# A chunked attention, mixture and MLP kernel: the first block's norm in earlier ticks, its later steps placed one by one, and a new order of the prologue

## The chip, the cores and the metric

The kernel runs on one core of one Trainium2 chip. The metric is the device time of one launch in microseconds, the median of several runs. The engines are named as in the profile: PE is TensorE (PEld its weight loads), DVE is VectorE, ACT is ScalarE, POOL is GpSimd, SP issues the DMAs.

## What is computed

The inputs are q, k, v of shape (8, 8, 576, 64) in float32, four experts' projections, a gate, a gain and two MLP weights in float64. Three stages follow each other; the reference, cut to what matters:

```python
# 1: attention within chunks of 64 positions, 8 heads
scores = 1/sqrt(64) * q_c @ k_c^T;  attn = softmax(scores);  x = attn @ v_c      # x: (8, 576, 512)
# 2: four single-head causal attention experts over 576 positions, top 2 of 4 weighted by a gate
logits = x @ w_gate;  w = softmax of the two largest
for e in range(4):
    a = softmax(causal(1/8 * (x @ wq[e]) @ (x @ wk[e])^T))
    out += (weight of e, or 0) * (a @ (x @ wv[e]) @ wo[e])
# 3: layer norm and MLP with a residual
xn = (out - mean) / sqrt(var + 1e-6) * g_ln
y = out + relu(xn @ w_ch1) @ w_ch2                                                # w_ch1: 512 x 2048
```

## The kernel before, in words

The 4608 rows are 36 tiles of 128 (`NT`). A **tick** `s` works on several tiles at once: the chunk attention of tile `s` (`chunk_scores`, `chunk_shift`, ...), the projections of a finished group of three tiles (`proj_group`), and the causal attention of tile `g = s - 6` in steps spread over three ticks. Ticks 6 to 36 do all of it, ticks 37 to 43 only what is left of the causal attention. Before tick 6 stands the **prologue**, the string `PRO` of L662, which loads the first six tiles and the projection weights, and keeps PE running with dummy products (`warm`, L92: `w40` and `w14`).

Every matmul operand of stages 2 and 3 is split in two float32r parts, a high one (a copy on ACT) and a low one (a subtraction on DVE or POOL), and three products are summed.

Within prologue and ticks nothing is scheduled: each engine gets its instructions in the order in which the code names them, and the code names them by the tables `PRO` and `PLAN` (L565), a letter for each step. For the steps of a tick: `S0`, `S1` scores (PE, L374), `D0`, `D1` mask and maximum (DVE, L392), `E0`, `E1` exp (ACT, L397), `L` sums (DVE, L405 to L407), `W` weighing (POOL, L414), and one tick later `T` transposes (PE, L425) whose results ACT and DVE copy to `pTa` (L427, L429), one more tick later `O` values (PE, L444), `Z` and `z` the high and low part of their result (`zh`, ACT and `zl`, DVE, both L447), `Y` the output projection (PE, L454, which needs `zl`), `y` its copy and store to the DRAM tile `xs`. `P` is a step of the projections (PE, L260 and L287), `a` and `v` their high and low parts. In the prologue: `c` chunk scores, `N` shift (DVE), `n` exp (ACT), `R` sums (DVE), `r` scaling (POOL), `K`, `k` transposes and their copy, `V` values, `H`, `X` the high and low part of x; `c`, `h`, `l`/`p` before a part's name (`v1`, `k0`, ...) load a half of a weight, make its high part, and its low part on DVE or POOL.

Stage 3 works by blocks of four tiles with seven products for each pair of hidden chunks (a Strassen-like scheme, L838). Block 0's input is made by `norm` for each of its two halves (load from `xs`, statistics, square root, scaling in place, transposes into `xt`), `sums` (four differences of quarters of `xt`), `operand` (seven operands `x7_1` to `x7_7`, high on ACT at L795, low on DVE at L796) and `split_w1` for the first two weight tiles `w1u0` and `w1u1` (L739, L740). All of that is one generator, `begin` (L799), of which the letter `F` in ticks 37 to 42 takes the next step. Block 1's norm stands later in the code, outside any table; its instructions are placed by the scheduler and land in ticks 38 to 40, as soon as block 0's transposes have freed the two buffers `xc`. The first five products of stage 3 (`lead_in`) are the letter `M` in ticks 42 and 43. From there to the end PE runs products back to back.

Buffers that matter here: `ps` and `pss` are PSUM pools with two and three buffers; `xc` has two.

Of the kernel before, what the change touches and what calls it, by code (L numbers as in the profile page):

```python
# [22 lines left out]
def tile_kernel(ctx, tc, dims, qkt, vt, wqt, wkt, wvt, wo, g_ln, w_ch1, w_ch2, out):  # L23
# [638 lines left out]
    PRO = ("L0 w40 c0 w14 L1 N0 cv1 c1 L2 cv0 n0 N1 R0 r0 n1 c2 hv1 K0 R1 r1 k0 N2 V0 hv0 lv1 n2 L3 K1 R2 c3 H0 k1 d2 V1 "  # L662
# [42 lines left out]
    E_ = mybir.EngineType  # L705
    ALL = {E_.PE, E_.DVE, E_.Activation, E_.Pool}
    with tc.manual_schedule(engines=ALL):
        for op in PRO.split():
            start_up(op)
        nc.sync.dma_start(gk, g_ln.rearrange("(f p) -> p f", p=128))  # L710
        bg(LA)
        for s in range(LA, MID):
            tick(s)
    early.close()

# [528 lines left out]
```

## Time and profile before

| | us |
|---|---|
| median of 3 runs | 1206.86 (1206.44 to 1208.41) |
| the profiled execution | 1207.36 |
| its span | 1205.6 |
| PE busy in the span | 1175.2 (97%) |
| DVE, ACT, POOL busy | 908.5, 579.3, 284.3 |
| prologue: to the first scores of tick 6 | 41.26 |
| tick 38 ends on PE at | 427.96 |
| first product of stage 3 on PE at | 466.31 |

The profiled execution is 0.5 us above the median. Its span is 1.76 us short of its time. PE is busy nearly throughout, so the table is to be read by stages: the gaps of PE are at the beginning (first 75 us) and between 428 and 466 us. A busy PE isn't always at its peak: its clock is granted at one of two levels, and the views by window give the mean (1.00 is 2.4 GHz, 0.50 is 1.2 GHz).

### The profile page before, as it was taken

Reading aid. Unit: us, or ns where it says so; the run is one execution under the profiler, and the core shown is the slowest. Engines: PE = TensorE matmul, PEld = TensorE weight load, DVE = VectorE, ACT = ScalarE, POOL = GpSimd, SP = SyncE. Lnnn points to the kernel's source line nnn. Section 1 sums busy time; section 2 is a strip of 40 time slices with the busy share of each in tenths; the row PEclk is TensorE's granted clock in tenths of the full one; section 3 lists DMA queues with packets and bytes.
Section 4 is the critical chain, followed back from the end, with each engine's and each line's share of the span. In section 5 each row is a group of like instructions: output and inputs, shape, how many; then the busy total and the mean of one; then the engine's idle time right before and its main releaser. Section 6 shows DMA issues by size and latency. Waiting matters only on the chain.

```text
span 1205.6 us, 29148 instructions
## 1 busy us (share of the span) xinstructions
PE 1175.2 (97%) x11838; PEld 1126.8 (93%) x11838; DVE 908.5 (75%) x1827; ACT 579.3 (48%) x1099; POOL 284.3 (24%) x490
## 2 busy tenths in 40 slices
PE   8899999999999979999999999999999999999998
PEld 7789988998988867999999999999999999999998
DVE  5888888888888785877765776556898777877782
ACT  3565656666666675534433433345454334333340
POOL 3345444535454362122111211210000000000000
PEclk8999999999999989999999999999999999999999
DMA  7343434343431233765555555558875455545521
GB/s 271 120 135 128 148 113 146 130 131 133 143 128 52 77 114 118 277 194 191 172 173 179 170 182 182 182 148 273 285 247 172 143 169 162 158 158 160 172 80 44
DMA packets 95733, 191.69 MB, mean 159 GB/s; under 512 B 8560, under 2 KB 41840, under 8 KB 94704
## 3 DMA queue, kind: packets, MB, share of 16 engines
q1 hardware_dynamic: 95600, 189.83, 48.1%
q8 instruction: 93, 1.52, 0.5%
q14 instruction: 40, 0.33, 0.1%
HBM read 118.50 MB, written 71.30 MB: 157 GB/s over the span
## 4 chain that ended last, share of the span: by engine, by line
PE 86%; DVE 9%; ACT 2%; POOL 1%; issue 1%; DMA 1%; ACTq 0%; POOLq 0%; DVEq 0%
PE bb L838 17%; PE bb L1069 16%; PE ad L838 13%; PE ad L1069 12%; PE pp L260 7%; PE oa_ps L444 3%; PE pv L287 3%; PE y_ps L454 3%; PE tp L425 3%; PE sp L374 3%; PE tp L778 1%; PE sx_ps L168 1%; PE pT_ps L194 1%; DVE P L392 1%; PE sx_ps L204 1%
## 5 line engine op out<-in xcount | busy, mean ns | idle before, releaser
L838 PE MATMUL bb<-x,w1u 128*128 128x256 f32 x1728 | 217.4, 281 | 0.0
L838 PEld LDWEIGHTS bb<-x,w1u 128*128 128x128 f32 x1728 | 209.8, 188 | 0.7 <-ACT y L459 0.2
L838 PE MATMUL ad<-x,w1u 128*128 128x256 f32 x1296 | 169.5, 281 | 0.0
L838 PEld LDWEIGHTS ad<-x,w1u 128*128 128x128 f32 x1296 | 159.6, 188 | 0.1
L1069 PE MATMUL bb<-w2u,hn 128*128 128x256 f32 x640 | 120.3, 280 | 0.6 <-DVE hn L1017 0.6
L1069 PE MATMUL bb<-w2u,hx 128*128 128x256 f32 x584 | 109.5, 281 | 0.9 <-DVE xr L1080 0.9
L414 POOL TENSOR_SCALAR P<-P,l 128x128 f32<-128x128 f32 (+8 forms) x144 | 93.5, 666 | 60.6 <-DVE l L407 53.1
L397 ACT ACTIVATE P<-P,nm 128x128 f32<-128x128 f32 (+8 forms) x144 | 87.0, 607 | 23.5 <-DVE nm L392 22.5
L1069 PEld LDWEIGHTS bb<-w2u,hn 128*128 128x128 f32 x640 | 97.1, 189 | 0.8 <-DVE hn L1017 0.8
L1069 PEld LDWEIGHTS bb<-w2u,hx 128*128 128x128 f32 x584 | 89.1, 189 | 1.0 <-PE bb L1069 1.0
L499 POOL TENSOR_TENSOR cv<-cv 128x512 f32<-128x512 f32 x16 | 27.3, 1705 | 235.5 <-DVE cv L495 219.2
L1069 PE MATMUL ad<-w2u,hn 128*128 128x256 f32 x440 | 80.7, 281 | 0.0
L1069 PE MATMUL ad<-w2u,hx 128*128 128x256 f32 x432 | 78.7, 281 | 0.0
L529 POOL TENSOR_TENSOR cw<-cw 128x128 f32<-128x128 f32 x128 | 64.9, 527 | 56.9 <-issue 39.9
L796 DVE TENSOR_TENSOR x<-xt,x 128x512 fp32r<-128x512 f32 x63 | 56.3, 899 | 17.1 <-ACT x L795 17.1
L1069 PEld LDWEIGHTS ad<-w2u,hn 128*128 128x128 f32 x440 | 65.8, 189 | 0.0
L1069 PEld LDWEIGHTS ad<-w2u,hx 128*128 128x128 f32 x432 | 64.9, 189 | 0.0
L392 DVE CUSTOM_DVE_ANT_0 P<-sp,mcaus 128x128 f32<-128x128 f32 (+7 forms) x128 | 60.2, 517 | 2.3 <-POOL P L414 1.1
L425 PE MATMUL tp<-ident,P 128*128 128x128 f32 x464 | 59.3, 278 | 2.0 <-POOL P L414 1.7
L444 PE MATMUL oa_ps<-pTa,vg 128*64 128x128 f32 x928 | 59.8, 279 | 1.4 <-DVE pTa L429 1.2
L188 POOL TENSOR_TENSOR pc<-pc,lc 128x512 f32<-128x512 f32 x34 | 35.6, 1046 | 103.6 <-DVE lc L184 56.4
L425 PEld LDWEIGHTS tp<-ident,P 128*128 128x128 f32 x464 | 52.6, 143 | 6.2 <-POOL P L414 1.9
(364 smaller groups left out, 2825.0 us busy)
## 6 DMA issues: line engine op xcount, KB each, us to landing
qk<-in_qk SPq DMA_DIRECT2D x35, 512.0 KB, 4.5
raw<-in_w_ch SPq DMA_DIRECT2D x32, 512.0 KB, 3.8
hx<-hd SPq DMA_DIRECT2D x28, 512.0 KB, 4.2
hn<-hd SPq DMA_DIRECT2D x25, 512.0 KB, 4.2
vb<-in_v SPq DMA_DIRECT2D x36, 256.0 KB, 4.5
xs<-y SPq DMA_DIRECT2D x36, 256.0 KB, 2.1
xc<-xs SPq DMA_DIRECT2D x18, 512.0 KB, 4.4
hd<-p SPq DMA_DIRECT2D x36, 256.0 KB, 4.2
```

The costliest lines, as they stand in the source:

```text
L260: nc.tensor.matmul(pp, a[:, f, ws], b_[:, f, :], start=(f == 0 and n == 0), stop=(f == KF - 1 and n == 2))
L287: nc.tensor.matmul(pv, a[:, f, cs], b_[:, f, :], start=(f == 0 and n == 0), stop=(f == KF - 1 and n == 2))
L374: nc.tensor.matmul(sv[:, si, :cn], x[r, ep, qc], y[r, ep, c0:c0 + cn], start=first, stop=last)
L392: nc.vector.tensor_tensor_reduce(dst, src, mk, -1.0, -3.0 * NEG, OP.add, OP.min, nm[:, e2:e2 + 1])
L397: nc.scalar.activation(pe, pe, AF.Exp, bias=nm[:, e2:e2 + 1], scale=-1.0, accum_out=l[:, e2:e2 + 1])
L414: nc.gpsimd.tensor_scalar(pe, pe, sums_[g][:, ep, e2:e2 + 1], 1.0, OP.mult, OP.mult)
L425: nc.tensor.transpose(tp[:, i, :], P[ep][e2][:, kt * 128:(kt + 1) * 128], ident)
L444: nc.tensor.matmul(o_ps[e2 * HD:(e2 + 1) * HD, ep, :], vg[:, gk % GT, e * HD:(e + 1) * HD], pT[:, e * n + kt, :], start=(kt == 0), stop=(k ...
L529: nc.gpsimd.tensor_tensor(w[:, o, :], w[:, x, :], w[:, y, :], op)
L796: nc.vector.tensor_tensor(t[:, 1], tsum[i], f32(t[:, 0]), OP.subtract)
L838: nc.tensor.matmul(out[:, p], w[:, kt, a, WI[i], :], x[:, b_, kt, :], start=(start and p == 0 and kt == 0 and q == 0), stop=False, skip_gr ...
L1069: ins = nc.tensor.matmul(to[:, t], x[:, c, ts], w2u[i][:, w, half * 4 + c, :], start=start, stop=False, skip_group_check=True)
```

## The change

The change has five parts.

1. **Norm of block 0.** Its load, statistics and scaling are steps `i0` and `i1` in ticks 34 to 36, its transposes in tick 38. A pool `sc` that lives throughout holds the two `xc` buffers; early on they hold halves of the weights v, k and o.
2. **The later steps of block 0**, one letter each in ticks 38 to 43: `u` a difference, `h` and `l` an operand's high and low part, `g` and `m` the high and low part of a half of `w1u0` or `w1u1`. A `P` at the end is POOL, otherwise DVE. Before, POOL made the four differences and the four low halves of `w1u0`, `w1u1`; now it makes one difference, two of those halves (both of `w1u0`) and the low parts of operands 6 and 1, and DVE the rest.
3. **Other orders** for ticks 34 to 43 (three more tables).
4. **A new prologue**: `w28` instead of `w40` ahead of the first scores, the first two tiles' scores one after the other, then `w12`, `w16` and later `w6` (62 dummies in all instead of 54), other places for weights and projections; weights are held in whole tiles.
5. **q/k by pairs**: the host stacks q and k within a pair of heads, so that each half of the first tile's load is one piece of a row.

Ticks 6 to 33, and everything after tick 43, keep their instructions in their order on PE, DVE, ACT and POOL. On SP the loads of block 0's `xc` now stand far ahead, in ticks 9 and 10, since the two halves that they read from `xs` are stored by then; block 1's loads of `xc` stand where they stood, behind the store of tick 37's result and ahead of `w1u0`.

```diff
-        raw = se.tile([128, 2 * VW], F32, name="wraw", bufs=6)[:, :src.size() // 128]
+        if c not in held:
+            held[c] = se.tile([128, 4 * VW], F32, name="wraw") if c == "q" else sc.tile([128, 4 * VW], F32, name="xc", bufs=2)
+        raw = held[c][:, half * 2 * VW:half * 2 * VW + src.size() // 128]
...
-        "38": "F O S0 S1 D1 Z D0 Q E0 z P a F E1 a L v W Y F F F v T P a v G1 y",
+        "38": "O S0 Z S1 D0 i0 i1 D1 E0 z Q P a E1 u7P u5V v a L v T P u6V a v h7 W Y G1 y",
...
+        "34": "S0 i1 S1 C D0 B E0 D1 O N H i0 E1 Z B B n T P X z B a R Y v r y K L P i1 a k B W B v B i0",
...
-    PRO = ("L0 w40 c0 w14 L1 N0 cv1 c1 L2 cv0 n0 N1 R0 r0 n1 c2 hv1 K0 R1 r1 k0 N2 V0 hv0 lv1 n2 L3 K1 R2 c3 H0 k1 d2 V1 "
+    PRO = ("L0 w28 L1 c0 cv0 c1 N0 N1 n0 n1 R0 R1 cv1 w12 r0 hv1 hv0 w16 L2 r1 c2 K0 N2 ck0 k0 n2 K1 L3 cq0 ck1 V0 k1 "
...
-        xc = sx.tile([128, 2, DM], F32, name="xc", bufs=2)
+        xc = sc.tile([128, 4 * VW], F32, name="xc", bufs=2)[:, :2 * DM].rearrange("p (a b) -> p a b", a=2)
...
+    def begin(op):
+        c, n = op[0], int(op[1])
+        eng = nc.gpsimd if op[-1] == "P" else nc.vector
+        if c == "i":
+            step(started.setdefault(n, norm(0, n)))
+        elif c == "u":
+            difference(0, n, eng)
+        elif c == "h":
+            operand_high(0, n)
+        elif c == "l":
+            operand_low(0, n, eng)
+        elif c == "g":
+            w1_high(n, int(op[2]))
+        elif c == "m":
+            w1_low(n, int(op[2]), eng)
...
-    put("qk", np.stack([heads(np.asarray(inputs[n])) for n in "qk"], axis=2).reshape(B * S // 128, 128, -1))
+    put("qk", np.stack([heads(np.asarray(inputs[n])) for n in "qk"], axis=3).reshape(B * S // 128, 128, -1))
```

What the tables make of it is shown at three places. First ACT in the prologue, before (`pc` is exp, `wvh`, `wkh` high parts of weights, `pTc` a copy of transposes, `xTh` a high part of x):

```order
L178 ACTIVATE pc<-pc 128x512 x2
L146 ACTIVATE wvh<-wraw 128x520
L196 ACTIVATE pTc<-pT_ps 128x512
L146 ACTIVATE wvh<-wraw 128x520
L178 ACTIVATE pc<-pc 128x512
L213 ACTIVATE xTh<-x_ps 128x4x128
```

and now, where both halves of `wvh` stand ahead of the first copy of transposes, and the high parts of the first two tiles behind the second:

```order
L185 ACTIVATE pc<-pc 128x512 x2
L153 ACTIVATE wvh<-xc 128x520 x2
L203 ACTIVATE pTc<-pT_ps 128x512
L185 ACTIVATE pc<-pc 128x512
L203 ACTIVATE pTc<-pT_ps 128x512
L153 ACTIVATE wkh<-xc 128x512
L220 ACTIVATE xTh<-x_ps 128x4x128 x2
```

Two tiles now go through the same steps side by side. Second, DVE from the masks of tick 40 to the copy of the transposes of that tick, before (`P,nm` is the mask step, `x_7` and so on low parts of operands):

```order
L392 ISA P,nm<-sp,mcaus 128x448
L392 ISA nm 128x1
L796 TENSOR_TENSOR x_7_7246<-xt,x_7_7246 128x512
L447 TENSOR_TENSOR zl<-oa_ps,zh 128x256
L796 TENSOR_TENSOR x_6_7254<-xt,x_6_7254 128x512
L796 TENSOR_TENSOR x_2_7257<-xt,x_2_7257 128x512
L796 TENSOR_TENSOR x_5_7268<-xt,x_5_7268 128x512
L796 TENSOR_TENSOR x_3_7273<-xt,x_3_7273 128x512
L796 TENSOR_TENSOR x_4_7276<-xt,x_4_7276 128x512
L429 COPY pTa<-tp 128x512
```

and now:

```order
L399 ISA P,nm<-sp,mcaus 128x448
L399 ISA nm 128x1
L741 TENSOR_TENSOR w1u_7114<-w1u_7114 128x896
L454 TENSOR_TENSOR zl<-oa_ps,zh 128x256
L813 TENSOR_TENSOR x_2_7242<-xt,x_2_7242 128x512
L741 TENSOR_TENSOR w1u_7114<-w1u_7114 128x896
L813 TENSOR_TENSOR x_3_7260<-xt,x_3_7260 128x512
L813 TENSOR_TENSOR x_7_7070<-xt,x_7_7070 128x512
L436 COPY pTa<-tp 128x512
```

Five low parts between `zl` and the copy have become three and a half weight tile; operands 4 and 5 moved behind, 1 and 6 to POOL. Third, POOL in ticks 39 to 41, before:

```order
L328 TENSOR_TENSOR wg<-ex,den 128x12
L414 TENSOR_SCALAR P<-P,l 128x320 x4
L386 MEMSET P 128x64 x2
L740 TENSOR_TENSOR w1u_7100<-w1u_7100 128x896 x2
L386 MEMSET P 128x64 x2
L740 TENSOR_TENSOR w1u_7102<-w1u_7102 128x896 x2
L414 TENSOR_SCALAR P<-P,l 128x448 x4
```

and now:

```order
L335 TENSOR_TENSOR wg<-ex,den 128x12
L741 TENSOR_TENSOR w1u_7112<-w1u_7112 128x896
L421 TENSOR_SCALAR P<-P,l 128x320 x4
L393 MEMSET P 128x64 x4
L813 TENSOR_TENSOR x_6_7179<-xt,x_6_7179 128x512
L813 TENSOR_TENSOR x_1_7161<-xt,x_1_7161 128x512
L421 TENSOR_SCALAR P<-P,l 128x448 x4
```

One half of `w1u0` stands ahead of the weighing of tick 39, two operands behind it, and the second half behind the weighing of tick 40.

## Rows read from the trace of the kernel before

**Rows 1.** PE's waits: line waited for, us in total, times, longest
```profile
PE y_ps L454 <- DVE zl L447: 7.2, 3, 4.1
...
PE x_ps L204 <- ACT pTc L196: 2.1, 3, 0.7
...
PE tp L425 <- POOL P L414: 1.7, 1, 1.7
```

**Rows 2.** Windows: stretch, length, busy of PE, PEld, DVE, ACT, POOL, PEclk, DMA
```profile
13.00:21.00 8.00, 5.17 (x106) 4.26 (x107) 7.00 (x15) 3.92 (x8) 3.41 (x3) 0.57 0.96 342
41.26:70.00 28.74, 25.74 (x326) 23.28 (x320) 25.17 (x76) 16.72 (x48) 13.29 (x23) 0.94 0.38 124
370.00:428.00 58.00, 58.00 (x628) 52.67 (x628) 42.90 (x138) 37.62 (x91) 24.85 (x47) 1.00 0.26 85
428.00:466.30 38.30, 27.75 (x235) 22.07 (x235) 34.49 (x86) 26.83 (x58) 23.74 (x35) 0.87 0.35 125
436.00:441.00 5.00, 5.00 (x32) 3.50 (x33) 4.95 (x23) 4.97 (x10) 1.09 (x2) 0.66 0.60 229
446.00:451.00 5.00, 5.00 (x19) 4.11 (x18) 5.00 (x3) 1.99 (x6) 5.00 (x5) 0.53 0.00 0
```

**Rows 3.** Timeline of PE in the prologue: start, us, instruction, [idle before <-releaser]
```profile
1.12 7.36 PE L97 MATMUL wp<-wz 128*128 128x256 bf16 x40 [1.12 <-DVE wz L90]
...
9.04 1.70 PE L97 MATMUL wp<-wz 128*128 128x256 bf16 x14
...
15.14 1.11 PE L194 MATMUL pT_ps<-ident,pc 128*128 128x128 f32 x4 [2.97 <-POOL pc L188]
...
21.23 0.37 PE L287 MATMUL pv<-wvh,xTl 128*128 128x260 f32 x1
...
41.26 0.33 PE L374 MATMUL sp<-kWh,ql 64*128 64x128 f32 x2
```

**Rows 4.** Timeline of DVE in the prologue: the second tile's shift
```profile
11.44 0.69 DVE L172 TENSOR_REDUCE nmc<-s_ps 128x8 f32<-128x512 f32 x1 [0.84 <-PE s_ps L168]
```

**Rows 5.** Timeline of PE, ticks 38 to 42
```profile
422.50 1.91 PE L778 MATMUL tp<-ident,xc 128*128 128x128 f32 x16
...
445.58 0.77 PE L454 MATMUL y_ps<-woh,zl 128*128 128x512 f32 x1 [4.06 <-DVE zl L447]
...
466.31 1.68 PE L838 MATMUL bb<-x,w1u 128*128 128x256 f32 x12
```

**Rows 6.** Timeline of DVE, ticks 39 to 41
```profile
435.24 0.42 DVE L447 TENSOR_TENSOR zl<-oa_ps,zh 128x256 fp32r<-128x256 f32 x1
...
442.97 2.12 DVE L796 TENSOR_TENSOR x<-xt,x 128x512 fp32r<-128x512 f32 x1
...
445.35 8.44 DVE L796 TENSOR_TENSOR x<-xt,x 128x512 fp32r<-128x512 f32 x5
```

**Rows 7.** Groups of DVE, 427 to 467 us: count, busy us, mean ns, idle before
```profile
L796 DVE TENSOR_TENSOR x<-xt,x 128x512 fp32r<-128x512 f32 x7 | 11.2, 1650 | 0.0
```

**Rows 8.** Line 796 over the whole span: minimum, median, maximum ns
```profile
L796 DVE TENSOR_TENSOR x<-xt,x x63: 670/693/2574, 437.0 to 809.2; 128x512 fp32r<-128x512 f32 x63
```

**Rows 9.** Groups of POOL, 427 to 467 us
```profile
L740 POOL TENSOR_TENSOR w1u<-w1u 128x896 fp32r<-128x896 f32 x4 | 9.4, 2380 | 0.0
L786 POOL TENSOR_TENSOR xt<-xt 128x512 f32<-128x512 f32 x1 | 1.3, 1282 | 0.0
```

**Rows 10.** Line 740 over the whole span, on DVE, which shares it with POOL
```profile
L740 DVE TENSOR_TENSOR w1u<-w1u x12: 1076/1085/1402, 462.8 to 498.6; 128x896 fp32r<-128x896 f32 x12
```

**Rows 11.** Groups of ACT: loads of the square root's table
```profile
L762 ACT ACT_TABLE_LOAD x3 | 3.8, 1283 | 0.1
```

**Rows 12.** SP's waits, 427 to 440 us: line waited for, us in total, times, longest
```profile
SPq L730 <- POOL wg L328: 4.2, 1, 4.2
```

**Rows 13.** Line 730 from 427 to 440 us: the loads of `w1u0` and `w1u1`
```profile
L730 SPq DMA_DIRECT2D w1u<-w1d x2: 526/540/555, 429.4 to 434.2; - x2
...
DMA to landing us min/median/max: 5.1/5.1/5.1
```

More of the change, by code (lines that the diff above doesn't have):

```diff
@@ L66, in tile_kernel @@
     late = ExitStack()
+    sc = ctx.enter_context(tc.tile_pool(name="sc", bufs=1, side="right"))
     se = early.enter_context(tc.tile_pool(name="se", bufs=1, side="right"))
@@ L651, in tick @@
                 start_up(op)
+            elif op[0] in "iuhlgm" and len(op) > 1:
+                begin(op)
             elif do.get(op):
@@ L703, in start_up @@
             prologue[c](int(n))
[L705 to L714, printed above, removed]
     outf = out.rearrange("b s d -> (b s) d")
@@ L793, in operand @@
-    def operand(j, i):
-        t = sx.tile([128, 2, 2, 256], F32R, name=f"x7_{i}")
-        nc.scalar.activation(t[:, 0], tsum[i], AF.Copy)
-        nc.vector.tensor_tensor(t[:, 1], tsum[i], f32(t[:, 0]), OP.subtract)
-        x7[j, i] = t
-    def begin():
-        n0, n1 = norm(0, 0), norm(0, 1)
-        step(n0)
-        step(n1)
-        for _ in range(4):
-            yield
-        step(n0)
-        step(n1)
-        yield
-        step(n0)
-        step(n1)
-        yield
-        step(n0)
-        yield
-        step(n1)
-        yield
-        s7 = sums(0, nc.gpsimd)
-        step(s7)
-        yield
-        step(s7)
-        yield
-        for i in (1, 7, 6, 2, 5, 3, 4):
-            operand(0, i)
-            yield
-            if i in (1, 7):
-                split_w1(i // 7, nc.gpsimd)
-                yield
+        a, b = xt[j][:, 0], xt[j][:, 1]
@@ new lines, in difference, with sums @@
+        t = {5: xt[j][:, 2, b1], 6: xt[j][:, 2, b2], 7: xt[j][:, 3, b1], 4: xt[j][:, 3, b2]}
+        x, y = {5: (b[:, b1], a[:, b1]), 7: (b[:, b2], b[:, b1]), 6: (b[:, b2], t[5]), 4: (a[:, b2], t[6])}[m]
+        if m > 4:
+            tsum.update({1: a[:, b1], 2: a[:, b2], 3: b[:, b2]})
+        eng.tensor_tensor(t[m], x, y, OP.subtract)
+        tsum[m] = t[m]
+    def sums(j):
+        for ms in ((5, 7), (6, 4)):
+            for m in ms:
+                difference(j, m)
+            yield
@@ L879, in lead_in @@
             made.add((0, i))
-            assert len(halved) > 1
+            assert len(halved) > 3 and (0, i) in ready
             yield from group1_steps(0, i)
     lead = lead_in()
-    beg = begin()
-    def fill():
-        next(beg, None)
+    E_ = mybir.EngineType
+    ALL = {E_.PE, E_.DVE, E_.Activation, E_.Pool}
+    with tc.manual_schedule(engines=ALL):
+        for op in PRO.split():
+            start_up(op)
+        nc.sync.dma_start(gk, g_ln.rearrange("(f p) -> p f", p=128))
+        bg(LA)
+        for s in range(LA, MID):
+            tick(s)
+    early.close()
+    sx = ctx.enter_context(tc.tile_pool(name="sx", bufs=1, side="right", reuse_waits="tile"))
     with tc.manual_schedule(engines=ALL):
         for s in range(MID, TAIL):
-            tick(s, fill)
+            tick(s)
     while gates:
@@ L903, in tile_kernel @@
         for s in range(TAIL, NT + LA):
-            tick(s, fill)
+            tick(s)
     keys.close()
@@ L911, in tile_kernel @@
         for s in range(NT + LA, NT + LA + 2):
-            tick(s, fill)
-    while next(beg, 0) != 0:
-        pass
+            tick(s)
     late.close()
@@ L963, in take @@
             return t, fresh.pop(t)
-        return t, POOLS[t].tile([128, 4, 256], F32R, name="h" + t, tag=t, bufs=2 if t == "xc" else 1)
+        if t == "xc":
+            return t, sc.tile([128, 4 * VW], F32R, name="hxc", tag=t, bufs=2)[:, :1024].rearrange("p (a b) -> p a b", a=4)
+        return t, POOLS[t].tile([128, 4, 256], F32R, name="h" + t, tag=t)
     def give(h):
```

76 lines of the change are left out of this document (44 added, 32 removed), and 20 rows, old and new, of tables (PLAN, PRO).

## The prediction

> **What bounds the kernel now.** TensorE. It is busy 1175.2 of 1205.6 us, so a change that leaves its products alone can only take away its gaps and the stretches at the lower clock. The view of its waits comes first, since it names who releases it [rows 1]: 7.2 us for `zl` in three waits, 2.1 for the copies of chunk transposes in three, 1.7 for POOL's weighing. Next come the windows [rows 2], for where the gaps lie. From 370 to 428 us (ticks 35 to 38) PE is busy all 58.0 us at full clock, with VectorE at 42.9 and ScalarE at 37.6: nothing is to be won there, and 15 us of VectorE stand free. From 428.0 to 466.3 PE is busy 27.75 of 38.30, so it idles 10.55, while VectorE is busy 34.5. Two 5 us windows there ran at a mean clock of 0.66 and 0.53 though PE was always busy, which lost 5 x 0.34 + 5 x 0.47 = 4.05 us. Gaps and clock together give 14.6 us, the most that ticks 39 to 42 can return. The ticks 6 to 8 (41.26 to 70.00) hold 3.0 us of gaps with VectorE at 25.2 of 28.7.
>
> The prologue is read on PE's timeline [rows 3]: 40 dummies to 8.41, 14 more from 9.04 for 1.70 (0.12 each), a gap of 2.97 at 15.14 for POOL's scaling, first value product at 21.23, first scores of tick 6 at 41.26. Behind the gap the clock is 0.57 in the mean of 13 to 21 us [rows 2]. VectorE's shift of the second tile waited 0.84 for its scores [rows 4], which stand behind the 14 dummies.
>
> The late gaps have a cause on VectorE. PE's output projection of tick 40 waits 4.06 for `zl` [rows 5], and `zl` stands behind one low part of an operand that took 2.12; five more took 8.44 behind it [rows 6]. All seven in this stretch took 11.2, mean 1.65 [rows 7], while the median of that line over the span is 0.693 [rows 8]. What was different is POOL: it ran four low halves of weights at 2.38 each meanwhile [rows 9]. A VectorE instruction and a POOL instruction with two SBUF inputs slow each other here, VectorE's by 1.65 / 0.693 = 2.4. The Trainium skill, GPSIMD Engine Reference, section 1. Specifications, gives GpSimd's SBUF interfaces as shared with VectorE, with contention against VectorE instructions that have two SBUF inputs; the trace agrees (1.65 against 0.693). On VectorE a half weight takes 1.085 [rows 10] where POOL needs 2.38.
>
> **The change, part by part.** The sum is made on the profiled 1207.36.
>
> *Prologue.* 12 fewer leading dummies at 0.12 bring the first scores 1.4 earlier, if they are there by then (the first load is now one piece per row; a later landing would eat it: 0 to -1.4, I take -1.4, since PE had work up to 8.41 that nothing needed). The second tile's scores no longer stand behind 14 dummies, so the shift's 0.84 goes. The gap of 2.97 for POOL is filled by 28 dummies, which hides what remains of it and keeps the clock up: the 8 us at a mean of 0.57 could give 8 x 0.43 = 3.4 if all were on the path. Most is not: value products need the weights' high parts, now all ahead of the transposes' copies on ScalarE. I take 0.35 from it: first value product at 21.23 - 1.4 - 0.84 - 0.35 = 18.6. Behind that, two tiles side by side leave two of three waits for the transposes' copies without cause: 2 x 0.7 = 1.4 [rows 1]. Sum -4.0, so tick 6 starts near 37.2. Ends: -1.4 (the dummies alone) and -6.0 (with 2 us of the clock). The 6 dummies further back cost under 1 us at 0.12 each and stand in a wait.
>
> *Ticks 34 to 38.* The same norm runs two ticks earlier, inside one stretch where PE had no gap and VectorE 15 us to spare. ScalarE loads the square root's table at 1.28 each [rows 11] at new places; with ScalarE at 37.6 of 58 this is hidden unless an exp that PE needs stands right behind. SP's loads of `xc` now stand in ticks 9 and 10 behind the stores they read; a store's landing delays the next tile's loads there, which are a tick ahead. Price +0.5, from 0 to +2 (two loads of a table that show half each, and some).
>
> *Ticks 39 to 42.* (i) Block 0's transposes stood behind the projections and the output projection of tick 38, at 422.50 [rows 5]; now right behind its second scores, near 417.5, the length of those (an estimate from PE's queue), 5 us earlier. So the buffers `xc` come free, and block 1's norm, which stands in VectorE's queue ahead of `zl` of tick 39, is through earlier. The last value projection, with the logits, also comes ahead of the output projection instead of behind it (about 1.5 earlier). I walk `zl` from 435.24 [rows 6] to about 432.5; it is then bound by the values of tick 39 themselves, which end near 431 if PE goes through its queue without a gap. That is -2.5; 0 to -4.
> (ii) `zl` of tick 40. Ahead of it stand four masks as before, then a half of `w1u1` at 1.08 [rows 10] in place of the low part of 2.12, and neither the four scalings of block 1 nor one low part remain in the way. It also needs `w1u1` loaded. Before, SP's load waited 4.2 for POOL's last step of the gate [rows 12], was issued at 434.2 and landed 5.1 later [rows 13]. With the logits earlier the gate ends near 431.5 and the half lands near 437.1; its high part on ScalarE, for which I take no more than the 1.08 of the low part (an estimate), and the 1.08 give 439.3, then `zl` at 439.5. Before it began at about 445: -5.5 in all, so -3.0 beyond (i). Without a wait of 4 us the clock should not fall a second time, which is in the next term. Ends 0 and -4.
> (iii) Behind `zl`, the copy of the transposes of tick 40 stands behind three low parts and half a weight in place of five low parts that took 8.44. POOL runs two operands beside them at about 1.28 each (as its difference of the same size, [rows 9]), so one or two of the three run slow: 3 x 0.69 + 1.08 + about 1.6 = 4.8. -3.6; ends -1.5 and -5.
> (iv) The last transposes' wait for POOL's weighing (1.7, [rows 1]) stays.
> Sum -9.1, so -9; ends -4 and -13. Stage 3's first product comes at 466.31 - 4 + 0.5 - 9 = 453.8. Behind it PE has no gap, and nothing is moved.
>
> Total: -4.0 + 0.5 - 9.0 = -12.5, 1207.36 - 12.5 = 1194.9. The profiled run is 0.5 above the median, so 1194.4.
>
> **Rivals.**
> A. The walk above: 1194.4, with its own range of 1190 to 1199.
> B. **Contention stays.** POOL keeps two-input work in ticks 40 and 41 (two operands, half of `w1u0`), and VectorE gets more of it (the differences, `w1u1`). If all low parts still take 1.65 and the halves of `w1u1` 2.6 (1.085 x 2.4), five operands cost 5 x 0.96 and two halves 2 x 1.5 more than clear ones, 7.8 in all, of which (iii) already holds 1.6: +6, 1200.4. For it: rows 7 to 9. Against it: POOL's low halves were 9.4 us in one string, now its string behind the weighing is 2.6. By the rule of the Trainium skill, GPSIMD Engine Reference, section 1. Specifications, this would be the likelier of the two.
> C. **The prologue gives only the dummies.** The 62 dummies are more than the 54 before, and what PE wins ahead of tick 6 is waited for again in ticks 6 to 8, where VectorE is busy 25.2 of 28.7 [rows 2]. Then -1.4 in place of -4.0: 1197.0. For it: VectorE's own gap ahead of tick 6 was 0.84; against it: its queue also gets an earlier start.
> D. **The load of `w1u1` holds VectorE**, the slower side. In the new order the half of `w1u1` stands ahead of `zl` of tick 40; whatever VectorE has behind it (that `zl`, operands, the copy `pTa`) waits for the landing. Each us that it lands after 437.1 is one of PE's. Landing as before, at 434.2 + 5.1 = 439.3, costs 2.2, and 1196.6, still inside A. Slower than 1209.3 needs 15 us more, a landing at 452: the gate would have to end on POOL 10 us later and the load take 10 instead of 5.1. In the rows the load's whole wait was one step of POOL, which has less ahead of it now.
> E. B and C together, with ticks 34 to 38 at their upper end: 1194.4 + 6 + 2.6 + 1.5 = 1204.5, no change.
>
> **How the numbers follow.** A difference of 0.2% (2.4 us) is about what a measurement of this kernel can tell from none. Chances: A 0.60, B 0.15, C 0.12, D 0.06, E 0.07. The likeliest is A, 1194.4. Lower end: prologue -6, ticks -13 and a median 0.5 lower, 1187.9, so 1188; upper end 1202, which takes in C and B with 1.6 to spare, and leaves out D, E and tails of A. Faster: A, B, C and a bit of E, 0.88. Within 0.2%: most of E, 0.06. Slower: D, 0.06.
>
> **What would show it.** In the changed kernel's profile: first scores near 7.0 us, no gap of over 1 us between 10 and 16 and a clock over 0.9 in 13 to 21; tick 6 near 37.2 (39.9, or new gaps up to 70: C). PE still gapless in ticks 35 to 38. `zl` of tick 39 near 432.5 less the prologue's gain of 3.5, PE's waits for `zl` under 2 us in sum in place of 7.2, no window at half clock from 428 on; VectorE's low parts there near 0.9 in the mean (1.6 and more: B). A VectorE wait for a DMA at `w1u1`: D. First product of stage 3 near 453.8. I am wrong if that product comes after 460, or if it comes in time and the end doesn't move with it.

## The result, and the profile after

The changed kernel takes 1196.4 us, median of 4 runs (1195.63 to 1197.66), against 1207.09 in the same comparison: ratio 0.9911, interval 0.9894 to 0.9928, 10.7 us faster. A second comparison later gave 1195.8 and 0.9903 (0.9889 to 0.9916). The forecast was 1194.4, with 1188 to 1202 as its range.

The profiled execution has a span of 1194.7 (before 1205.6). First PE's waits, the lines that answer to [rows 1] (line waited for, us in total, times, longest):

```profile
PE y_ps L461 <- DVE zl L454: 3.3, 3, 2.7
PE pT_ps L201 <- DVE l L412: 2.0, 1, 2.0
PE bb L848 <- ACT w1u L736: 1.3, 1, 1.3
PE pT_ps L201 <- POOL pc L195: 1.3, 2, 0.8
...
PE bb L848 <- DVE w1u L741: 0.7, 1, 0.7
PE pv L294 <- ACT pTc L203: 0.7, 1, 0.7
```

The wait for `zl` fell from 7.2 to 3.3, one of the three waits for transposes' copies is left, the wait for the last weighing is gone, and two waits for a weight tile in stage 3 are new. PE's timeline (start, us, instruction, idle before and its releaser) gives the marks, first in the prologue, for [rows 3]:

```profile
1.12 5.42 PE L98 MATMUL wp<-wz 128*128 128x256 bf16 x28 [1.12 <-DVE wz L91]
6.48 0.69 PE L175 MATMUL s_ps<-qk 64*64 64x64 f32 x32
7.75 0.69 PE L175 MATMUL s_ps<-qk 64*64 64x64 f32 x32 [0.57 <-DMA qk<-in_qk]
8.37 3.23 PE L98 MATMUL wp<-wz 128*128 128x256 bf16 x28
...
17.78 0.36 PE L294 MATMUL pv<-wvh,xTl 128*128 128x260 f32 x1 [0.17 <-DVE xTl L220]
...
37.43 0.33 PE L381 MATMUL sp<-kWh,ql 64*128 64x128 f32 x2
```

and then in ticks 38 to 42, for [rows 5]:

```profile
416.26 1.97 PE L786 MATMUL tp<-ident,xc 128*128 128x128 f32 x16
...
431.85 0.50 PE L461 MATMUL y_ps<-woh,zl 128*128 128x512 f32 x1 [0.43 <-DVE zl L454]
...
438.62 0.50 PE L461 MATMUL y_ps<-woh,zl 128*128 128x512 f32 x1 [2.69 <-DVE zl L454]
...
455.02 1.67 PE L848 MATMUL bb<-x,w1u 128*128 128x256 f32 x12
```

First value product 21.23 to 17.78, tick 6 41.26 to 37.43, first product of stage 3 466.31 to 455.02. The windows (stretch, length, busy of PE, PEld, DVE, ACT, POOL, PEclk, DMA share, GB/s), for [rows 2]:

```profile
13.00:21.00 8.00, 7.05 (x190) 5.97 (x191) 5.13 (x11) 6.21 (x12) 6.00 (x6) 1.00 1.02 366
41.26:70.00 28.74, 26.32 (x359) 23.18 (x359) 25.76 (x78) 16.79 (x45) 16.05 (x25) 0.94 0.34 117
366.00:424.00 58.00, 57.17 (x613) 50.84 (x612) 44.74 (x144) 37.00 (x90) 23.02 (x44) 1.00 0.19 67
426.70:455.00 28.30, 24.67 (x235) 20.32 (x235) 23.80 (x74) 24.47 (x54) 19.14 (x29) 0.94 0.47 168
435.00:440.00 5.00, 2.31 (x20) 1.83 (x19) 4.43 (x10) 4.65 (x10) 5.00 (x5) 0.91 0.15 59
440.00:445.00 5.00, 4.53 (x29) 3.60 (x27) 3.18 (x7) 4.08 (x11) 4.39 (x8) 0.74 0.00 0
```

The prologue's clock is now 1.00 where it was 0.57. Ticks 39 to 42 take 28.3 us instead of 38.3, with 3.6 us of gaps instead of 10.6, though the clock still falls once behind the wait of 2.69. VectorE there, for [rows 6 and 7], as its timeline and its groups between 425 and 457 us:

```profile
431.38 0.42 DVE L454 TENSOR_TENSOR zl<-oa_ps,zh 128x256 fp32r<-128x256 f32 x1
...
436.94 1.30 DVE L741 TENSOR_TENSOR w1u<-w1u 128x896 fp32r<-128x896 f32 x1 [0.33 <-ACT w1u L736]
438.16 0.41 DVE L454 TENSOR_TENSOR zl<-oa_ps,zh 128x256 fp32r<-128x256 f32 x1
...
443.49 0.69 DVE L436 COPY pTa<-tp 128x512 f32<-128x512 f32 x1 [1.52 <-ACT pTa L434]
```
```profile
L813 DVE TENSOR_TENSOR x<-xt,x 128x512 fp32r<-128x512 f32 x4 | 2.9, 743 | 0.0
```

The low parts take 0.743 in the mean in place of 1.65. GpSimd's weighing of tick 39 got slower beside VectorE's low parts and halves: four pieces in 4.66 us. Before, beside masks and scalings, they took 2.41 (the first line is of the kernel before):

```profile
439.91 2.41 POOL L414 TENSOR_SCALAR P<-P,l 128x320 f32<-128x320 f32 x4 [5.70 <-DVE l L407]
434.68 2.10 POOL L741 TENSOR_TENSOR w1u<-w1u 128x896 fp32r<-128x896 f32 x1 [3.96 <-ACT w1u L736]
436.77 4.66 POOL L421 TENSOR_SCALAR P<-P,l 128x320 f32<-128x320 f32 x4
```

To see where the 10.9 us of span went, I followed how far each step stands ahead of the kernel before, at marks up to which PE has done the same products in both kernels:

| mark on PE | before | after | ahead |
|---|---|---|---|
| first scores of tick 6 | 41.26 | 37.43 | 3.83 |
| output projection of tick 16 | 162.38 | 158.61 | 3.77 |
| first scores of tick 32 | 345.81 | 342.59 | 3.22 |
| first scores of tick 34 | 372.60 | 369.38 | 3.22 |
| first scores of tick 36 | 393.76 | 391.26 | 2.50 |
| second scores of tick 38 | 417.02 | 415.83 | 1.19 |
| first product of stage 3 | 466.31 | 455.02 | 11.29 |
| end of the span | 1205.6 | 1194.7 | 10.9 |

So the prologue gained 3.8, ticks 16 to 18 took 0.6 of it, ticks 34 to 38 took 2.0, ticks 39 to 42 gained 10.1, and 0.4 was given back behind the first product of stage 3.

### The profile page after: what moved, and what is told of

It reads as the page before. It is cut to its first block, busy times and chain, and to the rows that moved or that the text cites. A ratio compares the mean times of both kernels' runs of the same rounds, so it can differ in the third digit from the quotient of the medians.

```text
span 1194.7 us, 29142 instructions
## 1 busy us (share of the span) xinstructions
PE 1171.1 (98%) x11846; PEld 1122.3 (94%) x11846; DVE 901.7 (75%) x1830; ACT 579.2 (48%) x1099; POOL 278.2 (23%) x487
## 3 DMA queue, kind: packets, MB, share of 16 engines
q8 instruction: 93, 1.52, 0.5%
## 4 chain that ended last, share of the span: by engine, by line
PE 85%; DVE 8%; DMA 2%; ACT 2%; issue 1%; POOL 0%; SPq 0%; ACTq 0%; DVEq 0%; POOLq 0%
PE bb L848 17%; PE bb L1086 16%; PE ad L848 13%; PE ad L1086 12%; PE pp L267 7%; PE oa_ps L451 4%; PE y_ps L461 3%; PE tp L432 3%; PE pv L294 3%; PE sp L381 3%; PE tp L786 1%; DMA w1u<-w1d 1%; PE sx_ps L175 1%; PE pT_ps L201 1%; DVE P L399 1%
## 5 line engine op out<-in xcount | busy, mean ns | idle before, releaser
L813 DVE TENSOR_TENSOR x<-xt,x 128x512 fp32r<-128x512 f32 x61 | 48.3, 794 | 17.0 <-ACT x L809 17.0
```

The costliest lines, as they stand in the source:

```text
L813: eng.tensor_tensor(t[:, 1], tsum[i], f32(t[:, 0]), OP.subtract)
```

## Experiments

The theory: GpSimd's two-input work beside VectorE's, and the place of block 0's steps, set the time of ticks 39 to 42; the prologue's gain adds to it. The rivals: the low parts are slow for another reason; the prologue's gain is taken back later. Two stretches are compared below: the **late stretch**, from the second scores of tick 38 to the first product of stage 3 (before 49.3, after 39.2, the changed kernel's second profile 39.8; three further kernels with the same orders there 39.8 to 40.4), and **ticks 32 to 35**, from the first scores of tick 32 to those of tick 36 (before 47.95, after 48.67). In ticks 32 and 33 nothing is changed and the lead stays at 3.22, so the second stretch measures the new orders of ticks 34 and 35. Two expectations below call its ends the scores of ticks 34 and 37; I had counted the scores of a wide tile, which come in two sets, as two ticks.

The late part of the change alone, with the old prologue, was not run: its 10.1 us are read from the marks.

**The measure: the changed kernel again.**

> The changed kernel once more, as the measure for the other runs beside it: 1196 to 1198. Its profile shows how much of a stretch differs between two executions of one kernel: I expect tick 6 within 0.8 us of 37.4, and the stretch from the first scores of tick 39 to the first product of stage 3 within 1 us of 28.3.

1195.8. Tick 6 at 37.46, ticks 39 to 42 (from the first scores of tick 39) 28.9 in place of 28.3. So a difference of 0.6 in a stretch is noise between two executions. But at the output projection of tick 15 this execution was 1.4 ahead of the first one (145.86 and 147.30). That is the clock; the windows say why (columns as above; the first line is of the first profile, the others of this one):

```profile
55.00:60.00 5.00, 5.00 (x92) 4.33 (x91) 3.48 (x11) 3.47 (x12) 1.22 (x3) 0.81 0.65 209
55.00:60.00 5.00, 5.00 (x96) 4.59 (x93) 4.48 (x14) 4.43 (x13) 1.25 (x3) 1.00 0.82 258
180.00:185.00 5.00, 4.80 (x26) 4.22 (x25) 3.33 (x9) 2.63 (x7) 3.71 (x5) 1.00 0.05 17
```

Here the clock stayed up behind two waits for VectorE, of 1.95 us in tick 7 and 1.67 in tick 18 (one expectation below calls it tick 16; I had miscounted). In the first profile it fell behind the one in tick 7 (1.96). Both waits are there in the kernel before too (1.92 and 1.67).

**The new prologue alone, on the kernel before** (twice).

```diff
-    PRO = ("L0 w40 c0 w14 L1 N0 cv1 c1 L2 cv0 n0 N1 R0 r0 n1 c2 hv1 K0 R1 r1 k0 N2 V0 hv0 lv1 n2 L3 K1 R2 c3 H0 k1 d2 V1 "
+    PRO = ("L0 w28 L1 c0 cv0 c1 N0 N1 n0 n1 R0 R1 cv1 w12 r0 hv1 hv0 w16 L2 r1 c2 K0 N2 ck0 k0 n2 K1 L3 cq0 ck1 V0 k1 "
...
```

> The kernel before with the new string of the prologue alone; ticks 34 to 43 and the layout of q and k as before. Theory (the prologue's gain is kept to the end): scores of tick 6 near 37.4 us in place of 41.26, every later step 3 to 3.8 earlier, time 1207.1 - 3.5 = 1203.6 (1203.0 to 1204.2). Rival (the late waits for VectorE take the gain back, since they hang on transfers and on GpSimd): first product of stage 3 less than 2 us earlier, time 1205 to 1207.

> The kernel before with the new prologue alone, a second time. Its first ten runs lay in two groups: 1203.5 to 1204.6 at a mean granted clock of 0.997, and 1208.8 to 1209.5 at 0.992 to 0.993. Theory (the prologue's gain of 3 us stays where the clock stays up; where it falls in ticks 7 and 16 it is given back): the same two groups, and in a profile without a fall in tick 16 the steps of ticks 34 to 38 stand 3 us ahead of the kernel before. Rival (the gain is lost in ticks 40 to 42 whatever the clock does): all runs within 1 of 1206.5.

0.9993 (0.998 to 1.0005), and 0.9994 (0.9985 to 1.0002) the second time: by the median 0.6 us, not clear of none, and not 3.5. Both medians (1206.2 and 1206.1) are the first expectation's rival's, and so is the first product of stage 3, 0.2 and 1.7 us earlier. The trace shows the gain and its loss. Tick 6 starts at 38.21 and 37.96, 3.1 and 3.3 ahead; the lead is still 3.0 to 3.3 at 162 us of the kernel before, and 1.3 and 1.7 at tick 34. Between lies a fall of the clock in tick 18, shown here for the second profile together with the one behind tick 7 (both read 0.66 in the first profile too):

```profile
55.00:60.00 5.00, 5.00 (x89) 4.27 (x86) 3.62 (x11) 3.15 (x10) 1.75 (x3) 0.66 0.61 210
180.00:185.00 5.00, 3.99 (x14) 3.98 (x15) 3.95 (x10) 3.37 (x9) 2.49 (x3) 0.66 0.19 72
```

The kernel before, in the profile shown, kept its clock in tick 18 (1.00 from 180 to 185 us). In the first profile another 1.2 went in the late stretch (50.5) and 1.6 behind it (740.9 us from the first product of stage 3 to the end, 739.3 before; 1.1 of this are longer waits for VectorE between 860 and 900 us), in the second nothing and 0.4. In the 21 runs the times go with the mean clock: 1203.5 to 1204.6 at 0.997 (four runs), 1204.8 to 1206.9 at 0.996 (four), 1205.6 to 1207.4 at 0.994 to 0.995 (six), 1208.8 to 1209.5 at 0.992 to 0.993 (the first ten only; 1207.5 to 1208.3 at 0.993 in the second eleven). So the two groups of the first ten are blurred the second time. The runs at 0.997 are some 3 us below the kernel before, but its own 35 runs beside them have none over 0.994, so this picks runs by their outcome and doesn't show that the gain is kept. Why the clock falls in tick 18 in one execution and not in another is open: what precedes it there has the same instructions in the same order. That this prologue makes it likelier isn't shown either: it fell there in 7 of the 12 profiles with the new prologue, and with the old one in the next kernel's (0.74 from 185 to 190 us) and not in the first.

**Contention alone, on the kernel before:** the low halves of `w1u0` and `w1u1` from GpSimd to VectorE.

```diff
-                split_w1(i // 7, nc.gpsimd)
+                split_w1(i // 7, nc.vector)
```

> The kernel before with the low halves of w1u0 and w1u1 on VectorE instead of GpSimd, nothing else. Theory (GpSimd's two-input work makes VectorE's low parts slow): the seven low parts of operands between 427 and 467 us fall from a mean of 1.65 us to 0.7, the copy of the transposes of tick 40 stands behind two halves at 1.1 and five low parts at 0.7 = 5.6 us in place of 8.44, time 1207.1 - 3 = 1204 (1203 to 1205). Rival (the low parts are slow for another reason, or VectorE is short of time as such): mean stays over 1.4, VectorE has 4.3 us more to do, time 1208 to 1211.

Groups of VectorE from 427 to 467 us (count, busy us, mean ns, idle before):

```profile
L740 DVE TENSOR_TENSOR w1u<-w1u 128x896 fp32r<-128x896 f32 x7 | 8.2, 1197 | 0.7 <-ACT w1u L739 0.7
L796 DVE TENSOR_TENSOR x<-xt,x 128x512 fp32r<-128x512 f32 x7 | 4.4, 678 | 0.0
```

The seven low parts take 0.678 in place of 1.65 in [rows 7], so the mechanism is as supposed: with no half weights on GpSimd beside them, VectorE does seven low parts and seven halves in 12.6 us, where seven low parts and two halves took 13.6 before. The late stretch fell from 49.3 to 46.9, the time by 0.15% (0.9985, 0.9976 to 0.9994; 1205.4), half of the 3 us expected. The wait for `zl` shows why:

```profile
436.26 0.50 PE L454 MATMUL y_ps<-woh,zl 128*128 128x512 f32 x1 [3.14 <-DVE zl L447]
446.93 0.70 PE L454 MATMUL y_ps<-woh,zl 128*128 128x512 f32 x1 [4.90 <-DVE zl L447]
```

It is longer, 4.90 in place of 4.06, since two halves of `w1u0` now stand ahead of the masks. So taking the contention away is worth 2.4 of the late gain of 10.1 in this order. The rest I put down to the orders; the norm's place, tried next, is some 3 of it, and no run isolates what is left.

**The norm in its old place,** tick 37, and the general orders back in ticks 34 to 36.

```diff
-        "37": "S0 D0 O Z S1 z E0 L P D1 a v E1 L1 P T Y a v W1 y W",
+        "37": "i0 i1 S0 D0 O Z S1 z E0 i0 i1 L P D1 a v E1 L1 P T Y a v W1 i0 i1 y W",
...
-        "34": "S0 i1 S1 C D0 B E0 D1 O N H i0 E1 Z B B n T P X z B a R Y v r y K L P i1 a k B W B v B i0",
...
```

> The changed kernel with block 0's norm in tick 37 and the general orders of ticks back in 34 to 36. Theory (the 2.0 us that the changed kernel loses between ticks 34 and 38 without a visible gap are the price of the norm and of the three tables): that loss falls to 0.5, scores of tick 38 about 1.5 earlier, and time 1 lower, unless the transposes then wait for the norm in tick 38. Rival (the loss lies in the tables of ticks 37 and 38): no change in that stretch, within 0.5 us.

Ticks 32 to 35 take 47.95, as before: the new tables, with the norm in them, cost 0.7 there. But from the first scores of tick 36 to the second of tick 38 it takes 25.3 us (after 24.6, before 23.3), and PE now waits for the norm:

```profile
414.86 1.97 PE L451 MATMUL oa_ps<-pTa,vg 128*64 128x128 f32 x32 [1.30 <-ACT y L466]
418.28 1.07 PE L783 MATMUL tp<-ident,xc 128*128 128x128 f32 x8 [0.61 <-DVE xc L774]
421.10 1.10 PE L783 MATMUL tp<-ident,xc 128*128 128x128 f32 x8 [1.75 <-DVE nm L399]
```

The late stretch is 42.6 in place of 39.2, and the time 1200.5 (0.994, 0.9925 to 0.9956), 4.7 more than the changed kernel's beside it (1195.8). From the first scores of tick 32 to the first product of stage 3 it takes 115.8 us in place of 112.4: moving the norm ahead, with the tables that go with it, is worth some 3 us net.

**Without the norm's work,** the orders unchanged.

```diff
+        if not j:
+            yield
+            yield
...
```

> The changed kernel with the statistics, the square root and the scaling of block 0 left out (load and transposes stay; the first four tiles of the MLP's input are not normalized). Theory (0.7 us between the scores of tick 34 and of tick 37 is the price of the norm's work, 1.3 behind it that of the orders of ticks 37 and 38): from the scores of tick 34 to those of tick 37 48.7 us in place of 49.5, the loss behind it stays at 1.3. Rival (the three tables' orders cost it): 49.5 still.

Ticks 32 to 35 take 48.66, as with the norm: the 0.7 there is the orders of ticks 34 and 35, as the rival had it. From the first scores of tick 36 to the second of tick 38 it takes 23.9 in place of 24.6 (before 23.3), so half of the loss there is the norm, whose scaling stands in tick 36, and half the orders. In sum 0.7 of the 2.0 us is the norm. That is more than executions differ by here: the eight other profiles with these orders lose 0.69 to 0.75 in the first stretch and 1.26 to 1.35 in the second. The time, 1196.5, is the changed kernel's.

**`zl` of tick 40 first.**

```diff
-        "40": "S0 D0 P S1 h2 D1 g10 O g01 Z h3 a m10V P g11 z E0 Y l2V m11V h4 E1 l3V l7V l6P T L l1P v W a y v",
+        "40": "S0 D0 P S1 h2 D1 O Z g10 g01 h3 a z m10V P g11 E0 Y l2V m11V h4 E1 l3V l7V l6P T L l1P v W a y v",
```

> The changed kernel with the values' high and low part (Z and z) of tick 40 ahead of the halves of w1u1 and w1u0 that stood ahead of them. Theory (PE's 2.7 us wait for zl in tick 40 is VectorE at the low half of w1u1, 1.3 us and a wait of 0.33 for its high part): zl 1.6 us earlier, the wait about 1, but the transposes behind it are then held by GpSimd's weighing, which ends at 441.4; time 1196.4 - 1.2 = 1195.2 (1194.5 to 1195.9). Rival (the masks and the scores ahead hold zl): wait over 2 us, time 1196.2 to 1196.8.

The wait for `zl` is 1.07 as forecast, but the time is 1198.6 (0.9931, 0.9918 to 0.9943), the late stretch 41.3. PE's timeline shows the shorter wait and what grew behind it:

```profile
437.35 0.50 PE L461 MATMUL y_ps<-woh,zl 128*128 128x512 f32 x1 [1.07 <-DVE zl L454]
439.94 0.55 PE L432 MATMUL tp<-ident,P 128*128 128x128 f32 x3 [0.27 <-POOL P L421]
441.85 0.55 PE L432 MATMUL tp<-ident,P 128*128 128x128 f32 x3 [1.36 <-POOL P L421]
443.89 0.61 PE L381 MATMUL sp<-kWh,ql 64*128 64x288 f32 x1 [1.17 <-ACT pTa L434]
```

The weighing holds the transposes, as I had it, and the clock then stays at 0.51 from 445 to 450, which I had not.

**The weighing of tick 39 first.**

```diff
-        "39": "P S0 O P D0 a E0 h1 G2 Z z S1 D1 h6 u4V T E1 a g00 G3 m00P L Y v v y W",
+        "39": "P S0 O P D0 a E0 h1 G2 Z z S1 D1 h6 u4V T E1 a g00 G3 L Y v v y W m00P",
```

> The changed kernel with GpSimd's low half of w1u0 behind the weighing of tick 39 instead of ahead of it. Theory (the transposes of tick 40 took 2.27 us for 12 since the weighing, 4.66 us for four pieces, ended only at 441.4): weighing ends near 439, transposes in 1.4 us, time 1196.4 - 0.7 = 1195.7 (1195.2 to 1196.1). Rival (PE's clock, which is low there, sets the 2.27): no change, 1196.2 to 1196.8.

1197.8 (0.9927, 0.9915 to 0.994), the late stretch 41.1. GpSimd and VectorE, their timelines:

```profile
433.71 2.05 POOL L421 TENSOR_SCALAR P<-P,l 128x320 f32<-128x320 f32 x4 [3.82 <-DVE l L414]
435.73 2.08 POOL L741 TENSOR_TENSOR w1u<-w1u 128x896 fp32r<-128x896 f32 x1
```
```profile
436.25 2.51 DVE L741 TENSOR_TENSOR w1u<-w1u 128x896 fp32r<-128x896 f32 x1 [0.46 <-ACT w1u L736]
```

The weighing is done in 2.05 instead of 4.66, at 435.8, but GpSimd's half weight now runs beside VectorE's, which takes 2.51 instead of 1.30, and PE waits 4.04 for the `zl` behind it. Neither the theory nor the rival had that.

**Both, and both with earlier transposes.** The first has the two edits above and no other.

> The changed kernel with both edits: zl of tick 40 ahead of the halves of w1u1, and GpSimd's weighing of tick 39 ahead of the half of w1u0. Theory (each edit alone moved the wait: with zl first the transposes waited for a weighing slowed by VectorE's two-input work, with the weighing first the two engines' half weights met and zl waited 4 us): both together leave neither, zl's wait is about 1, no wait for the weighing; but the copy of the transposes behind the halves now holds the values of tick 41 by 1 to 2 us; stretch 39 to 42 27 to 28.5 us, time 0 to 1.5 below the changed kernel's. Rival (the slow clock after any wait eats it): stretch 30, time 1 to 2 above.

```diff
-"... g11 z E0 Y l2V m11V h4 E1 l3V l7V l6P T L l1P v W a y v",
+"... g11 E0 Y T l2V h4 E1 L W m11V l3V l7V l6P l1P v a y v",
```

> As with both edits, and the transposes of tick 40 with their copies named right behind its output projection, ahead of three of the low parts. Theory: the copy is no longer held, PE has no wait over 1.2 us in ticks 40 and 41 and the clock stays up; stretch 39 to 42 25.5 to 27 us, time 1.5 to 3 below the changed kernel's. Rival (GpSimd and VectorE meet elsewhere, in ticks 41 and 42): first products of stage 3 wait for operands or halves, stretch 28 or more, no gain.

1199.8 (0.9934, 0.992 to 0.9947) and 1200.1 (0.9939, 0.9926 to 0.9951), late stretches 41.6 and 43.7: the rivals. With both edits the wait for `zl` is 1.06 and none is left for the weighing; instead the copies of the transposes on ScalarE stand behind four exps and a high part:

```profile
444.28 0.60 PE L381 MATMUL sp<-kWh,ql 64*128 64x288 f32 x1 [3.24 <-ACT pTa L434]
```

With the transposes named earlier the clock holds through the late ticks, but PE waits for the masks behind the halves and low parts, then for copies behind the sums:

```profile
447.07 0.40 PE L381 MATMUL sp<-kWh,ql 64*128 64x288 f32 x1 [2.83 <-DVE nm L399]
453.65 1.96 PE L451 MATMUL oa_ps<-pTa,vg 128*64 128x128 f32 x30 [1.73 <-DVE pTa L436]
```

In four tries the wait went from VectorE to GpSimd, to ScalarE and back. VectorE, ScalarE and GpSimd are busy 23.8, 24.5 and 19.1 of the 28.3 us in the changed kernel. No version here beats the changed kernel.

**The dummies.** First without the 34 behind the first scores, then with 40 ahead.

```diff
-    PRO = ("L0 w28 L1 c0 cv0 c1 N0 N1 n0 n1 R0 R1 cv1 w12 r0 hv1 hv0 w16 L2 r1 c2 K0 N2 ck0 k0 n2 K1 L3 cq0 ck1 V0 k1 "
-           "cq1 L4 V1 L5 R2 c3 hk0 pv0 H1 w6 r2 H0 pv1 K2 X0 X1 k2 P hq1 hq0 N3 a hk1 c4 V2 P v H2 lq0 pk0 co0 X2 lq1 "
+    PRO = ("L0 w28 L1 c0 cv0 c1 N0 N1 n0 n1 R0 R1 cv1 r0 hv1 hv0 L2 r1 c2 K0 N2 ck0 k0 n2 K1 L3 cq0 ck1 V0 k1 "
+           "cq1 L4 V1 L5 R2 c3 hk0 pv0 H1 r2 H0 pv1 K2 X0 X1 k2 P hq1 hq0 N3 a hk1 c4 V2 P v H2 lq0 pk0 co0 X2 lq1 "
```

> The changed kernel without the 34 dummies behind the first scores (w12, w16, w6); the 28 ahead of them stay. Theory (they hide the wait for GpSimd's scaling and keep PE's clock up): PE idles 3 us ahead of the first transposes of chunks, its clock is near half from 13 to 20 us as in the kernel before, tick 6 comes 1.5 to 3 later (39 to 40.4), time 1197.5 to 1199. Rival (what PE does there waits for ScalarE and VectorE anyway): tick 6 within 0.5 of 37.4, time 1195.5 to 1196.5.

The clock fell as expected, in windows of the prologue:

```profile
10.00:15.00 5.00, 3.64 (x64) 2.72 (x68) 3.72 (x9) 3.05 (x7) 3.33 (x3) 0.61 1.04 391
15.00:20.00 5.00, 4.87 (x104) 4.31 (x100) 2.88 (x7) 3.30 (x7) 3.54 (x3) 0.71 0.93 330
```

but tick 6 started at 37.97, only 0.5 later, nearly as the rival had it. The time, 1198.1 (0.9921, 0.9907 to 0.9935), is the theory's, about 2 above the changed kernel's; the profiled execution has both falls of the clock, in ticks 7 and 18, and the one in tick 18 is 1.1 of it. The 0.5 is too small, since tick 6 hangs on the second tile's load: in the seven profiles with all dummies in which PE waits for that load, tick 6 starts 29.6 to 29.7 us behind the second tile's scores, at 37.25 to 38.11. Here it is 30.6 behind them (37.97 less 7.39), so the fill is worth 0.9.

```diff
-    PRO = ("L0 w28 L1 c0 cv0 c1 N0 N1 n0 n1 R0 R1 cv1 w12 r0 hv1 hv0 w16 L2 r1 c2 K0 N2 ck0 k0 n2 K1 L3 cq0 ck1 V0 k1 "
+    PRO = ("L0 w40 L1 c0 cv0 c1 N0 N1 n0 n1 R0 R1 cv1 w12 r0 hv1 hv0 w16 L2 r1 c2 K0 N2 ck0 k0 n2 K1 L3 cq0 ck1 V0 k1 "
```

> The changed kernel with 40 dummies ahead of the first scores in place of 28. Theory of the prediction (each dummy is 0.12 us of the path): tick 6 comes 1.4 later, 38.8. Theory from the changed kernel's trace (PE waited 0.57 for the second tile's load at 7.75, which the 12 dummies would fill): 0.8 later, 38.2, time 1196.7. Rival (PE is waited for by nobody there): no change.

Tick 6 at 38.11, 0.7 later; 1197.7 (0.9921, 0.9908 to 0.9934). PE's timeline shows that the scores of both tiles follow without the wait of 0.57 for the load, and that the first transposes now wait for GpSimd's scaling:

```profile
7.14 1.48 PE L175 MATMUL s_ps<-qk 64*64 64x64 f32 x64
...
12.93 0.65 PE L201 MATMUL pT_ps<-ident,pc 128*128 128x128 f32 x4 [0.52 <-POOL pc L195]
```

That the 12 dummies are worth 0.7 isn't shown by this. In the eleven profiles with 28 dummies these took 4.5 to 6.1 us, and in the one with 6.07 (both edits, above) the first scores came at 7.12 and tick 6 at 38.10, as with 40 here. What the traces show is that first scores anywhere from 5.6 to 6.75 change nothing, since the second tile's load bounds what follows, and that those at 7.1 do. Why the dummies take longer in one execution than in another is open. The layout of q and k was not tried alone.

## Why the prediction was right, by its steps

**The sum.** 12.5 us were forecast and 10.7 measured, on the side forecast and by the mechanism named likeliest (A), with two terms whose parts were not as supposed. Its terms, measured between the two profiles:

| term | forecast | measured |
|---|---|---|
| prologue | -4.0 | -3.8 |
| ticks 6 to 33 | 0 | +0.6 |
| ticks 34 to 38 | +0.5 (0 to +2) | +2.0 |
| ticks 39 to 42 | -9 (-4 to -13) | -10.1 |
| behind | 0 | +0.4 |

The 0.6 of ticks 6 to 33 is no cost of the change: the kernel with the halves on VectorE, whose instructions are those of the kernel before up to there, lost 1.3 against the same profile, 1.1 of it by the clock in tick 18. The loads of block 0's `xc`, which I had put in ticks 9 and 10, were issued at 104.64, in tick 12, and the lead is 3.8 on both sides of them.

**Prologue.** Its sum was right in the two profiles compared, partly by luck: tick 6 starts at 37.25 to 38.11 in eight profiles with the changed prologue, and at 40.55 and 41.26 in two with the old one, so the gain lies between 2.4 and 4.0. Its parts were not right. The first value product came 3.45 earlier, not 2.6; what lies behind it gave 0.4, not 1.4: one wait of 0.7 for a copy is left, and where the rest went I did not follow. Of the 3.45, 2.9 lie ahead of the second tile's scores (10.67 to 7.75), where the sum had 1.4 + 0.84, and now their load bounds them, not the dummies; the fill, taken at 0.35, is worth 0.9 by the run without it. The new prologue alone gave 0.6 by the median: the price of a gain at tick 6 depends on whether the clock falls later, which the prediction did not see. In ticks 6 to 8 it read the gaps and passed over the clock.

**Rival C** put the loss of the prologue's gain in ticks 6 to 8. There it did not go: the changed kernel's lead is 3.8 at both ends of them. But its number, a prologue worth little by itself, was nearly what the run with the new prologue alone gave, by way of the clock in tick 18.

**Ticks 34 to 38.** The mechanism named (table loads, the norm's work) was 0.7 of the 2.0; the rest is the orders of these ticks, which the prediction had not priced. Gaps show only part of it: from the first scores of tick 34 to the second of tick 38 PE is busy 45.75 of 46.45 us, before 44.42 of 44.42, with 527 products in both. The other 1.3 us lie in the same products following each other more slowly, and why they do I did not follow. The number ended on the upper bound. (The stretch from 370 to 428 us, which the prediction calls ticks 35 to 38, is ticks 34 to 38: tick 34 begins at 372.60.)

**Ticks 39 to 42** came to the marks that were walked, counted from the second scores of tick 38, though not always by the cause named. (i) `zl` of tick 39 was forecast 15.5 us behind them (432.5 less 417.0) and came at 431.38 less 415.83 = 15.55. But it was not bound by the values of tick 39: VectorE had block 1's last two scalings, from 430.46, right ahead of it. (ii) `zl` of tick 40: 22.5 forecast, 22.3 measured, by the path named. The half of `w1u1` stood on it, with a wait of 0.33 for its high part, for which ScalarE had waited 0.35 for the load; so rival D was near, and its load landed when the forecast had it. (iii) The copy: 27.7 forecast, 27.7 measured, and this is luck: VectorE's low parts were done at 441.96, and the copy then waited 1.52 for ScalarE's, behind transposes that began at 440.93 and took 2.27. What held these was the slowed weighing (to 441.4) or PE's lower clock; the runs don't part the two. (iv) I had left the last transposes' wait for the weighing at 1.7; it was 0 in the first profile and 0.56 in the second. That is more than the 1.1 by which the stretch was better than forecast.

**What the signs said.** Four were wrong. PE's waits for `zl` sum to 3.3, not under 2, and the clock still falls from 435 to 445 us: PE itself arrives earlier at the projection of tick 40, so a wait of 2.69 stays, and the clock falls behind it. Where two windows lost 4.05 us to the clock before, the two above still lose 5 x 0.09 + 5 x 0.26 = 1.75. PE is not gapless in ticks 35 to 38 (it waits 0.41 for `zl` and 0.18 for the logits), and `zl` of tick 39 came at 431.38, not near 429, by what ticks 16 to 18 and 34 to 38 lost ahead of it.

**Rival B** fell: low parts at 0.743. The kernel before with the halves on VectorE shows that its mechanism is real there. The Trainium skill, GPSIMD Engine Reference, section 1. Specifications, names contention of GpSimd with VectorE instructions of two SBUF inputs; the runs agree (0.678 without, 1.65 with GpSimd's halves beside them). The change escapes it by placing the two engines' work side by side only in part, and the run with the weighing first shows what a collision costs (2.51 for 1.30).

**Behind the first product.** The 0.4 lost there can't be told from none: from the first product to the end the changed kernel takes 739.7 and 739.6 in its two profiles and others with the same orders there 738.6 to 740.4; the kernel before takes 739.3. The two new waits, at 480.6 and 481.8, are for the sixth weight tile, which ScalarE had itself waited 2.26 us to see landed:

```profile
480.63 0.39 PE L848 MATMUL bb<-x,w1u 128*128 128x256 f32 x1 [1.30 <-ACT w1u L736]
```

Where most of these 2.0 us is regained I did not follow.

## What to carry to other kernels

Count a late stretch from a mark on the bounding engine, and walk each engine's queue in its order: here that gave the three marks that mattered within 0.2 us, one of them by luck, so look up what each mark waited for before calling the walk right. When three engines are each busy over two thirds of a stretch, a wait that one edit removes is taken up by the next engine, and here the fix for each alone made the late stretch 1 to 2 us longer. A gain far ahead of the end should be checked at marks on the way, since a later fall of the clock can take it.

## What the runs showed of the hardware

- TensorE's granted clock can fall behind a wait of 1.7 to 2.0 us, and does so in some executions and not in others of the same kernel: the changed kernel had 1.00 from 55 to 60 us in one profile and a fall (0.81) in the other. By the lead at the marks behind them the fall in tick 7 cost 1.45 us and those in tick 18 1.1. What decides it is open. The Trainium skill, TensorE: Matmul & The Clock Gate, Part 1: The HAM clock gate, says of the warm-up that the chip watches activity in a window that runs free of the kernel, and that the same kernel therefore differs from run to run; that would fit the falls too, but no run here shows the window.
- GpSimd and VectorE slow each other both ways: VectorE's low parts took 1.65 us in the mean beside GpSimd's half weights and 0.678 without them, and four pieces of GpSimd's weighing, each a tensor times a value per partition, took 2.05 us beside masks and 4.66 beside two-input subtractions.
